# An FFT, mixing and feed-forward kernel: the first two chunks by halves of the features, eight weight blocks ahead, tables and third-stage inputs moved

## The chip, the cores and the metric

The kernel runs on one core of a Trainium2 chip. The metric is the device time of one launch in microseconds. PE is TensorE (PEld its weight loads), DVE is VectorE, ACT is ScalarE, POOL is GpSimd, SP is SyncE; SP, ACT and POOL each have a queue from which they issue DMAs in program order.

## The reference

```python
X = rfft(x, axis=1)                       # x: 8 batches, 3072 rows, 256 columns
Yr = Xr @ w_r - Xi @ w_i + b_r
Yi = Xr @ w_i + Xi @ w_r + b_i
Yr, Yi = soft_threshold(Yr, 0.01), soft_threshold(Yi, 0.01)
y = irfft(Yr + 1j * Yi, n=3072, axis=1)   # real, 8 x 3072 x 256
h = y.reshape(-1, 256) @ w_in             # 256 -> 2048
out = (h * tanh(softplus(h))) @ w_out     # 2048 -> 256
```

w_in and w_out arrive as float64.

## The kernel before

**Precision.** Each value of a product is split into a float32r part `hi` and a rest `lo`, and a product is three matmul passes (hi by hi, lo by hi, hi by lo). The split is one copy and one subtraction. float64 weights are read as raw words (`raw`) and turned into two such parts on DVE, in steps: the class `FromDouble` makes a block of 128 x 1024 values in nine DVE steps (lines 253 to 277), the last two of which run inside the next block's work. There are 16 blocks: eight of w_in (`w1(k, n)`, of features 512n to 512n+511) and eight of w_out (`w2(n)`, of feature blocks 2n and 2n+1).

**The transform, per batch.** Four stages pass through scratch memory in HBM:
- first stage, items a (7, two matmul steps each): tile `psa`, results `eva` stored;
- second stage, items b (12, `psb`, with a table `tt` from HBM) each followed by an item m (mixing by w_r and w_i, thresholds; two matmul steps, `psm` in batch 0, `psk` and `psp` later), results `y` stored;
- third stage, items c (13, `psc`), four input DMAs each;
- fourth stage, items f (12, `psf`, with a table `vt`), which give the feed-forward inputs `yh`, `yl` of one chunk for each pair of items.

`run_chain` is a generator that issues an item's `load`, table load `cload` and split `prep` some items ahead and gives back control after each matmul step; `cla` is how many items ahead the tables are. With `gap` set it also yields empty steps after a stage's loads and after its first preps.

**The feed-forward part.** 48 chunks (6 a batch) by 16 feature blocks make 768 steps t. `ffn1(t)` is six matmuls of 512 columns into `hp`, followed by Mish on ACT; `split_g` splits two steps' results into `gh` and `gl`; `ffn2(t - 4)` is eight matmuls into four accumulators `acc` of a chunk, which after 16 steps are added and stored. A chunk runs through all 16 feature blocks before the next one starts.

**The order.** It is written by hand, in program order per engine. Batch 0's transform runs first, with weight steps of DVE spread among its matmul steps (`PACE`, steps per matmul step by stage; `aux_steps` in `on_seg`, steps at a stage's start). Up to `N_EARLY` = 11 blocks, 97 steps, are made there, the rest at t 0 to 18. From t=0 on, each t also takes one step of `gen`, the next batch's transform up to its items f0 and f1, and of `extra`, a chain of one item f for the batch in hand, started at t%16 = 2 and 8. An empty step of `extra` leaves the t to `gen`; a matmul step does not. What is left of `gen` at a batch's last t is issued there in one go.

Before t=0 a job's weight load is issued on POOL from within an earlier job's steps, and its buffers go round among `raw`, `gl` and `ot` tiles. The loads of items c and f and of x are on SP; in batch 0 half of those of c are on POOL, and so is half of the stores of y.

Of the kernel before, what the change touches and what calls it, by code (L numbers as in the profile page):

```python
# [128 lines left out]
def fft_mix_ffn_kernel(ctx: ExitStack, tc: tile.TileContext, x, w_r, w_i, b_r, b_i, w_in, w_out,  # L129
# [147 lines left out]
            nc.vector.tensor_tensor(out=self.lo, in0=f32(self.high), in1=self.t, op=ALU.add)  # L277
            yield

    N_EARLY = 11  # L280

    def weight_jobs():
        def w1(k, n):
            sl = slice(n * 512, (n + 1) * 512)
            return (w_in.bitcast(I32)[k * 128:(k + 1) * 128, n * 1024:(n + 1) * 1024],
                    *(win[:, k, s, sl].rearrange("p (a c) -> p a c", a=2) for s in range(2)), False)

        def w2(n):
            return (w_out.bitcast(I32)[n * 256:(n + 1) * 256, :].rearrange("(k p) c -> p k c", p=128),
                    *(wout[:, 2 * n:2 * n + 2, s, :] for s in range(2)), True)  # L290

        order = [w1(0, 0), w1(1, 0), w1(0, 1), w1(1, 1), w2(0), w2(1), w1(0, 2), w1(1, 2), w2(2), w2(3),
                 w1(0, 3), w1(1, 3), w2(4), w2(5), w2(6), w2(7)]
        return [FromDouble(n, *a) for n, a in enumerate(order)]


# [399 lines left out]
    def run_chain(segs, ahead_n=3, ahead_a=2, cla=2, gap=0, hold=None, on_seg=None):  # L696


        for k, seg in enumerate(segs):
            while hold is not None and k == len(segs) - 1 and hold():  # L700
                yield None
            n = len(seg)
            at = [0, 0, 0]
            la, pla = (ahead_a, 1) if k == 0 and n == 7 else (ahead_n, 2)

            def ahead(i):
                for s, (d, f) in enumerate(((la, "load"), (cla, "cload"), (pla, "prep"))):
                    while at[s] < min(n, i + d):
                        getattr(seg[at[s]], f)()
                        at[s] += 1  # L710

            while at[1] < min(n, cla):
                seg[at[1]].cload()
                at[1] += 1
            while at[0] < min(n, la):
                seg[at[0]].load()
                at[0] += 1
            if on_seg is not None:
                on_seg(k)
            last = k == len(segs) - 1  # L720
            for _ in range(gap + (4 if k == 2 else 1 if last else 0) if gap else 0):
                yield None
            while at[2] < min(n, pla):
                seg[at[2]].prep()
                at[2] += 1
            for _ in range((2 if last or k == 1 else 1) if gap else 0):
                yield None
            for i in range(n):
                ahead(i + 1)
                for f in seg[i].mm:  # L730
                    tick()
                    f()
                    yield k
            tick()
# [2 lines left out]
    NCH = NB * 6  # L737
    s_t, g_t, acc = {}, {}, {}

    def ffn1(t):  # L740

        c, f = divmod(t, KFF)
        yh, yl = y_t[(c // 6, c % 6)]
        hp = ps_d.tile([128, 512], F32, tag="d", name="hp")
        n = 0
        for k in range(2):
            for s, m in ((0, yh), (0, yl), (1, yh)):
                nc.tensor.matmul(out=hp, lhsT=win[:, k, s, f * 128:(f + 1) * 128], rhs=m[:, k, :],  # L748
                                 start=n == 0, stop=n == 5)
                n += 1  # L750
        if t % 2 == 0:
            s_t[t // 2] = p_s.tile([128, 2, 512], F32, tag="s", name="s")
        nc.scalar.activation(out=s_t[t // 2][:, t % 2, :], in_=hp, func=ACTF.Mish)  # L753

    def split_g(q, early):
        s = s_t.pop(q)
        gh = p_g.tile([128, 2, 512], F32R, tag="gh", name="gh")
        gl = p_g.tile([128, 2, 512], F32R, tag="gl", name="gl", bufs=2)
        if early:
            nc.scalar.activation(out=gh, in_=s, func=ACTF.Copy)  # L760
        else:
            nc.vector.tensor_copy(out=gh, in_=s)  # L762
        nc.vector.tensor_tensor(out=gl, in0=s, in1=f32(gh), op=ALU.subtract)  # L763
        g_t[q] = (gh, gl)

    def ffn2(t):
        c, f = divmod(t, KFF)
        gh, gl = g_t[t // 2]
        if f == 0:
            acc[c] = [ps_o.tile([128, 2, 256], F32, tag="o", name=f"acc{k}") for k in range(4)]  # L770
        last = f == KFF - 1
        if last:
            ot = p_o.tile([128, 2, 2, 256], F32, tag="ot", name="ot")
        for k in range(4):
            b2, h = divmod(k, 2)
            p = acc[c][k]
            o = b2 * 256 + h * 128
            nc.tensor.matmul(out=p, lhsT=gh[:, t % 2, o:o + 128], rhs=wout[:, f], start=f == 0, stop=False)  # L778
            nc.tensor.matmul(out=p[:, 0], lhsT=gl[:, t % 2, o:o + 128], rhs=wout[:, f, 0], start=False, stop=last)  # L779
            if last:  # L780
                cor = p_w.tile([128, 256], F32, tag="cor", name="oc")
                nc.scalar.activation(out=cor, in_=p[:, 1], func=ACTF.Copy)  # L782
                nc.vector.tensor_tensor(out=ot[:, h, b2, :], in0=p[:, 0], in1=cor, op=ALU.add)  # L783
        if last:
            b, cc = divmod(c, 6)
            dst = out[b * SEQ:(b + 1) * SEQ].rearrange("(h a b2) c -> a h b2 c", h=2, b2=12)
            nc.sync.dma_start(out=dst[:, :, 2 * cc:2 * cc + 2, :].rearrange("a h b2 c -> a h (b2 c)"),
                              in_=ot.rearrange("p h b c -> p h (b c)"))
            acc.pop(c)
        if t % 2 == 1:  # L790
            g_t.pop(t // 2)


    with tc.manual_schedule():
# [22 lines left out]
        def aux_steps(m):  # L817
            for _ in range(m):
                if started[0] or n_aux[0] < 9 * N_EARLY - 2:
                    next(aux_gen, None)  # L820
                    n_aux[0] += 1

        def on_seg(k):
            if k == 1:
                top[0] = N_EARLY
                aux_load(4)
                setup_mix()
                aux_steps(6)
            elif k == 2:
                aux_steps(12)  # L830
            elif k == 3:
                aux_steps(10)

        PACE = (1.6, 0.9, 1.4, 2)
        first = chain(0)
        cnt = 0
        owed = 0.0
        for k in run_chain(first, ahead_n=6, ahead_a=3, cla=3, on_seg=on_seg):
            cnt += 1
            if cnt in (2, 6):  # L840
                aux_load(1 + (cnt > 2))
            if cnt == 8:
                load_mix()
                load_bias()
            if cnt == 11:
                for it in first[1][:3]:
                    it.cload()
            if cnt == 20:
                setup_u()
            if cnt == 57:  # L850
                for it in first[3]:
                    it.cload()
            if cnt > 4:
                owed += PACE[k]
            while owed >= 1:
                aux_steps(1)
                owed -= 1
# [9 lines left out]
        for t in range(NT + LAG):  # L867
            tt = t % NS
            b = t // NS
            if t == 0:  # L870
                aux_load(N_EARLY + 2)
            if t < 18:
                aux_steps(3)
            if t == 18:
                aux_steps(18)
                mix_gauss()
            if t < NT:
                if tt == 0:
                    gen = run_chain(chain(b + 1), gap=2, hold=lambda: hold[0]) if b + 1 < NB else None
                hold = [tt < 5 * KFF + 2]  # L880
                ffn1(t)
                c = tt // KFF
                if tt % KFF in (2, 8) and c < 5:
                    extra = run_chain([[item_f(b, 2 * c + 2 + (tt % KFF) // 8)]], gap=2)
            if t % 2 == 0 and t // 2 - 1 in s_t:
                split_g(t // 2 - 1, t < 18)
            did = None
            if extra is not None:
                did = next(extra, -1)
                if did == -1:  # L890
                    extra = did = None
            if did is None and gen is not None and t < NT:
                did = next(gen, -1)
                if did == -1:
                    gen = None
            if t < NT and tt == NS - 1 and gen is not None:
                hold = [False]
                for _ in gen:
                    pass
                gen = None  # L900
            if t >= LAG:
                ffn2(t - LAG)
# [26 lines left out]
```

## Time and profile before

| | |
|---|---|
| median of 3 runs | 2815.71 us (2812.26 to 2817.09) |
| profiled execution | 2812.9 us, span 2811.1 us |
| granted TensorE clock, mean | 0.987 |
| busy PE, DVE, ACT | 97%, 69%, 34% |
| first stage of batch 0 | 0 to 43 us |
| second | 43 to 106 us |
| third | 106 to 146 us |
| fourth | 146 to 158 us |
| first hp (t=0) | 158.19 us |

Stages are told apart by the lines of their instructions. A row of the timeline gives start and length in microseconds, engine, line, operation, tiles, and in brackets the idle time of that engine ahead of it and what ended it. PE's lengths overlap: the next matmul starts before the one before has ended. A row of the waits gives engine and tile, what was waited for, the sum in microseconds, the number of times and the longest.

### The profile page before, as it was taken

Reading aid. Unit: us, or ns where it says so; the run is one execution under the profiler, and the core shown is the slowest. Engines: PE = TensorE matmul, PEld = TensorE weight load, DVE = VectorE, ACT = ScalarE, POOL = GpSimd, SP = SyncE. Lnnn points to the kernel's source line nnn. Section 1 sums busy time; section 2 is a strip of 40 time slices with the busy share of each in tenths; the row PEclk is TensorE's granted clock in tenths of the full one; section 3 lists DMA queues with packets and bytes.
Section 4 is the critical chain, followed back from the end, with each engine's and each line's share of the span. In section 5 each row is a group of like instructions: output and inputs, shape, how many; then the busy total and the mean of one; then the engine's idle time right before and its main releaser. Section 6 shows DMA issues by size and latency. Waiting matters only on the chain.

```text
span 2811.1 us, 39281 instructions
## 1 busy us (share of the span) xinstructions
PE 2739.7 (97%) x14782; PEld 2333.5 (83%) x14782; DVE 1952.8 (69%) x3294; ACT 951.2 (34%) x1947; POOL 148.0 (5%) x274
## 2 busy tenths in 40 slices
PE   6779999999999999999999999999999999999999
PEld 5558888888888888888888888888888888888887
DVE  5788866778667776678766777567766778655553
ACT  4333333333333333333333333323333333333232
POOL 1400000000000000000000000000000000000000
PEclk9789999999999999999999999999999999999999
DMA  7643324333233323342233332433324333231000
GB/s 223 204 143 86 94 70 120 102 90 94 72 112 109 99 80 86 101 121 84 76 106 102 104 84 68 120 106 87 90 75 120 98 91 91 78 95 42 27 27 16
DMA packets 170388, 266.38 MB, mean 95 GB/s; under 512 B 22518, under 2 KB 67590, under 8 KB 170198
## 3 DMA queue, kind: packets, MB, share of 16 engines
q1 hardware_dynamic: 122806, 173.75, 20.6%
q0 software_dynamic: 33536, 64.95, 8.6%
q10 hardware_dynamic: 13856, 25.17, 3.1%
q8 instruction: 117, 1.92, 0.3%
q14 instruction: 73, 0.60, 0.1%
HBM read 163.10 MB, written 100.68 MB: 94 GB/s over the span
## 4 chain that ended last, share of the span: by engine, by line
PE 87%; DVE 5%; DMA 3%; SPq 2%; issue 1%; ACT 1%; POOL 0%; ACTq 0%; DVEq 0%; POOLq 0%
PE hp L748 35%; PE acc L778 23%; PE acc L779 12%; PE psp L518 4%; PE psa L345 2%; PE psc L626 2%; SPq L604 2%; PE psk L499 2%; PE psf L666 2%; PE psb L434 2%; DMA ld<-in_x_dram 1%; DMA ld<-s 1%; PE psf L667 1%; DVE lo L190 1%; PE psb L436 1%
## 5 line engine op out<-in xcount | busy, mean ns | idle before, releaser
L778 PE MATMUL acc<-wout,gh 128*128 128x512 f32 x3072 | 1115.7, 397 | 0.0
L748 PE MATMUL hp<-yh,win 128*128 128x512 f32 x3072 | 1082.1, 393 | 4.9 <-ACT yh L675 4.6
L753 ACT ACTIVATE s<-hp 128x512 f32<-128x512 f32 x768 | 458.5, 597 | 1368.7 <-PE hp L748 1283.3
L779 PE MATMUL acc<-wout,gl 128*128 128x256 f32 x3072 | 859.2, 280 | 0.0
L748 PEld LDWEIGHTS hp<-yh,win 128*128 128x128 f32 x3072 | 578.6, 188 | 137.4 <-ACT yh L675 4.8
L778 PEld LDWEIGHTS acc<-wout,gh 128*128 128x128 f32 x3072 | 576.6, 188 | 123.4 <-issue 6.0
L748 PE MATMUL hp<-yl,win 128*128 128x512 f32 x1536 | 604.1, 393 | 0.0
L779 PEld LDWEIGHTS acc<-wout,gl 128*128 128x128 f32 x3072 | 577.5, 188 | 16.3
L763 DVE TENSOR_TENSOR gl<-s,gh 128x1024 fp32r<-128x1024 f32 x384 | 470.5, 1225 | 65.3 <-PE acc L779 26.1
L762 DVE CAST gh<-s 128x1024 fp32r<-128x1024 f32 x376 | 258.7, 688 | 207.1 <-ACT s L753 207.1
L748 PEld LDWEIGHTS hp<-yl,win 128*128 128x128 f32 x1536 | 289.2, 188 | 35.0 <-DVE yl L676 0.4
L190 DVE TENSOR_TENSOR lo<-ld,hi 120x512 fp32r<-120x512 f32 (+3 forms) x390 | 269.7, 692 | 31.8 <-ACT hi L189 16.3
L187 DVE CAST hi<-ld 120x512 fp32r<-120x512 f32 (+2 forms) x367 | 154.7, 422 | 56.5 <-DMA ld<-s 55.5
L670 DVE TENSOR_TENSOR eo<-psf,cor 128x256 f32<-128x256 f32 x192 | 76.9, 422 | 117.5 <-ACT cor L669 116.8
L783 DVE TENSOR_TENSOR ot<-acc,oc 128x256 f32<-128x256 f32 x192 | 72.8, 420 | 98.2 <-ACT oc L782 98.2
L650 POOL DMA_DIRECT2D vt<-in_c_v_dram x96 | 52.5, 547 | 1609.4 <-PE psf L667 1261.1
L518 PE MATMUL psp<-wmix,xh 128*128 128x256 f32 x672 | 133.2, 281 | 0.0
L676 DVE TENSOR_TENSOR yl<-yt,yh 128x512 fp32r<-128x512 f32 x96 | 66.5, 693 | 67.1 <-ACT yh L675 67.1
L518 PEld LDWEIGHTS psp<-wmix,xh 128*128 128x128 f32 x672 | 109.1, 188 | 3.6
L675 ACT ACTIVATE yh<-yt 128x512 fp32r<-128x512 f32 x96 | 60.7, 632 | 145.4 <-DVE yt L673 145.4
L626 PE MATMUL psc<-hi,uu 120*120 120x512 f32 (+1 forms) x224 | 89.0, 412 | 17.2 <-ACT hi L189 14.8
L666 PE MATMUL psf<-vt,hi 128*128 128x256 f32 x384 | 95.4, 325 | 7.5 <-ACT hi L189 7.5
(114 smaller groups left out, 2630.5 us busy)
## 6 DMA issues: line engine op xcount, KB each, us to landing
ld<-s SPq DMA_DIRECT2D x185, 256.0 KB
tt<-in_c_t_dram POOLq DMA_DIRECT2D x104, 256.0 KB, 3.2
vt<-in_c_v_dram POOLq DMA_DIRECT2D x96, 256.0 KB, 3.0
out_dram<-ot SPq DMA_DIRECT2D x48, 512.0 KB
ld<-in_x_dram SPq DMA_DIRECT2D x90, 240.0 KB
s<-ev ACTq DMA_DIRECT2D x89, 240.0 KB
s<-y SPq DMA_DIRECT2D x330, 64.0 KB
ld<-s SPq DMA_DIRECT2D x350, 60.0 KB
```

Source lines behind the costliest of these rows:

```text
L187: nc.vector.tensor_copy(out=hi, in_=src)
L190: nc.vector.tensor_tensor(out=lo, in0=src, in1=f32(hi), op=ALU.subtract)
L518: nc.tensor.matmul(out=it.ps[:, ri * 256:(ri + 1) * 256], lhsT=m[:, c, 130 - ri * 128:258 - ri * 128], rhs=wmix[:, c, s, 2 * ri, :], start ...
L626: nc.tensor.matmul(out=ps[:K, sl], lhsT=uu[:K, var, s, :K], rhs=m[:K, sl], start=n == 0, stop=n == 2)
L666: nc.tensor.matmul(out=ps[:, p], lhsT=it.hi[:, q:q + 128], rhs=it.v[:, p], start=True, stop=False)
L670: nc.vector.tensor_tensor(out=eo[:, c], in0=ps[:, :, 0], in1=cor, op=ALU.add)
L748: nc.tensor.matmul(out=hp, lhsT=win[:, k, s, f * 128:(f + 1) * 128], rhs=m[:, k, :], start=n == 0, stop=n == 5)
L753: nc.scalar.activation(out=s_t[t // 2][:, t % 2, :], in_=hp, func=ACTF.Mish)
L762: nc.vector.tensor_copy(out=gh, in_=s)
L763: nc.vector.tensor_tensor(out=gl, in0=s, in1=f32(gh), op=ALU.subtract)
L778: nc.tensor.matmul(out=p, lhsT=gh[:, t % 2, o:o + 128], rhs=wout[:, f], start=f == 0, stop=False)
L779: nc.tensor.matmul(out=p[:, 0], lhsT=gl[:, t % 2, o:o + 128], rhs=wout[:, f, 0], start=False, stop=last)
```

## The change

- The first two chunks (t 0 to 31) take turns: features 0 to 7 of chunk 0, 0 to 7 of chunk 1, 8 to 15 of chunk 0, 8 to 15 of chunk 1. Both use a two-accumulator form of `ffn2`, with 12 matmuls of 256 columns and no addition at the end.
- Eight weight blocks (70 steps) are made ahead of t=0, in an order that holds all of features 0 to 7. The other 76 steps stand at t 0 to 25.
- In batch 0's transform tables are loaded five items ahead, not three.
- Items f2 and f3 of batch 0 form one chain at t=0, f4 and f5 one at t=24. Batch 1's chain starts at t=18 and takes one more step at every fifth t behind 26. The Gauss weights of later batches (`mix_gauss`) are made at t=30, not 18.
- In `run_chain` the third stage has two empty steps after its first preps, not one. The same line gives a chain of one single stage (the items f of `extra`) one empty step after its prep, not two.

```diff
-    N_EARLY = 11
+    N_EARLY = 8
-        order = [w1(0, 0), w1(1, 0), w1(0, 1), w1(1, 1), w2(0), w2(1), w1(0, 2), w1(1, 2), w2(2), w2(3),
-                 w1(0, 3), w1(1, 3), w2(4), w2(5), w2(6), w2(7)]
+        order = [w1(0, 0), w1(1, 0), w1(0, 1), w1(1, 1), w2(0), w2(1), w2(2), w2(3),
+                 w1(0, 2), w1(1, 2), w2(4), w1(0, 3), w1(1, 3), w2(5), w2(6), w2(7)]
...
-            for _ in range((2 if last or k == 1 else 1) if gap else 0):
+            for _ in range((2 if k else 1) if gap else 0):
                 yield None
...
+    def place(t):
+        if t < 2 * KFF:
+            q, r = divmod(t, KFF // 2)
+            return q % 2, q // 2 * (KFF // 2) + r
+        return divmod(t, KFF)
...
+    def ffn2_two(t, c, f, gh, gl, last):
+        if f == 0:
+            acc[c] = [ps_o.tile([128, 2, 256], F32, tag="o", name=f"acc{k}") for k in range(2)]
+        ot = p_o.tile([128, 2, 2, 256], F32, tag="ot", name="ot") if last else None
+        for b2 in range(2):
+            for h in range(2):
+                o = b2 * 256 + h * 128
+                p = acc[c][b2][:, h, :]
+                for n, (m, s) in enumerate(((gh, 0), (gh, 1), (gl, 0))):
+                    nc.tensor.matmul(out=p, lhsT=m[:, t % 2, o:o + 128], rhs=wout[:, f, s, :],
+                                     start=f == 0 and h == 0 and n == 0, stop=last and h == 1 and n == 2)
+            if last:
+                nc.scalar.activation(out=ot[:, :, b2, :], in_=acc[c][b2], func=ACTF.Copy)
+        return ot
...
-                aux_steps(6)
+                aux_steps(8)
             elif k == 2:
                 aux_steps(12)
             elif k == 3:
-                aux_steps(10)
-        PACE = (1.6, 0.9, 1.4, 2)
+                aux_steps(9)
+        PACE = (1.6, 0.45, 0.7, 2)
-        for k in run_chain(first, ahead_n=6, ahead_a=3, cla=3, on_seg=on_seg):
+        for k in run_chain(first, ahead_n=6, ahead_a=3, cla=5, on_seg=on_seg):
...
-                for it in first[1][:3]:
+                for it in first[1][:5]:
                     it.cload()
...
-            if t < 18:
-                aux_steps(3)
-            if t == 18:
-                aux_steps(18)
+            if t < 26:
+                aux_steps(2 if t < 8 else 4 if t < 16 else 3)
+            if t == 30:
                 mix_gauss()
             if t < NT:
-                if tt == 0:
+                if tt == (0 if b else 18):
                     gen = run_chain(chain(b + 1), gap=2, hold=lambda: hold[0]) if b + 1 < NB else None
...
-                if tt % KFF in (2, 8) and c < 5:
+                if t in (0, 24):
+                    extra = run_chain([[item_f(0, 2 + t // 12), item_f(0, 3 + t // 12)]], gap=2)
+                elif t >= 2 * KFF and tt % KFF in (2, 8) and c < 5:
                     extra = run_chain([[item_f(b, 2 * c + 2 + (tt % KFF) // 8)]], gap=2)
             if t % 2 == 0 and t // 2 - 1 in s_t:
-                split_g(t // 2 - 1, t < 18)
+                split_g(t // 2 - 1, t < 26)
+            if b == 0 and gen is not None and t % 5 == 4 and t > 26:
+                next(gen, None)
```

On POOL, in batch 0's second stage (numbers tell tiles apart; `tt` are tables, the first one here is block 2's; `s3<-y` are stores, `raw` is a weight load), before:

```order
L400 DMA tt_453<-in_c_t_dram 128x512
L400 DMA tt_517<-in_c_t_dram 128x512
L205 DMA uu_103<-in_c_u_dram 120x720
L564 DMA s3_164<-y_534 32x512 x2
L400 DMA tt_568<-in_c_t_dram 128x512
L564 DMA s3_164<-y_584 32x512 x2
L245 DMA raw_594<-in_moe_w_in_dram 128x1024
L400 DMA tt_619<-in_c_t_dram 128x512
```

and after:

```order
L400 DMA tt_408<-in_c_t_dram 128x512
L400 DMA tt_456<-in_c_t_dram 128x512
L400 DMA tt_519<-in_c_t_dram 128x512
L205 DMA uu_103<-in_c_u_dram 120x720
L564 DMA s3_164<-y_535 32x512 x2
L400 DMA tt_568<-in_c_t_dram 128x512
L564 DMA s3_164<-y_584 32x512 x2
```

Block 5's table (tt_619 before, tt_568 after) now stands behind one pair of stores instead of two and behind no weight load. In the third stage two `raw` stood between the loads of c on POOL before; after, one stands ahead of them all and two behind the stage's `vt`.

On PE, at item f10 in a later batch (`psf` is its product; `gh_7503` before and `gh_7607` after are the halves of the same two steps t), before:

```order
L778 MATMUL acc3_7510<-wout_110,gh_7503 128x512
L779 MATMUL acc3_7510<-wout_110,gl_7504 128x256
L748 MATMUL hp_7560<-yh_7021,win_109 128x512
L748 MATMUL hp_7560<-yl_7022,win_109 128x512
L748 MATMUL hp_7560<-yh_7021,win_109 128x512 x2
L748 MATMUL hp_7560<-yl_7022,win_109 128x512
L748 MATMUL hp_7560<-yh_7021,win_109 128x512
L666 MATMUL psf_7571<-vt_7452,hi_7527 128x256
L667 MATMUL psf_7571<-vt_7452,lo_7528 128x128
```

and after:

```order
L755 MATMUL hp_7643<-yl_7089,win_109 128x512
L755 MATMUL hp_7643<-yh_7088,win_109 128x512
L666 MATMUL psf_7659<-vt_7556,hi_7631 128x256
L667 MATMUL psf_7659<-vt_7556,lo_7632 128x128
L666 MATMUL psf_7659<-vt_7556,hi_7631 128x256
L667 MATMUL psf_7659<-vt_7556,lo_7632 128x128
L666 MATMUL psf_7667<-vt_7556,hi_7631 128x256
L667 MATMUL psf_7667<-vt_7556,lo_7632 128x128
L666 MATMUL psf_7667<-vt_7556,hi_7631 128x256
L667 MATMUL psf_7667<-vt_7556,lo_7632 128x128
L797 MATMUL acc0_7611<-wout_110,gh_7607 128x512
```

psf stood behind the acc group that reads these halves first and behind one more hp; now it stands ahead of both, one t earlier. Its load's place on SP, behind the first three c items' loads, is the same.

On PE, at the end of batch 0 (from the end of item f1's psf of batch 1 to the next hp), before:

```order
L667 MATMUL psf_4804<-vt_4646,lo_4715 128x128
L778 MATMUL acc0_4573<-wout_110,gh_4706 128x512
L779 MATMUL acc0_4573<-wout_110,gl_4707 128x256
L778 MATMUL acc1_4574<-wout_110,gh_4706 128x512
L779 MATMUL acc1_4574<-wout_110,gl_4707 128x256
L778 MATMUL acc2_4575<-wout_110,gh_4706 128x512
L779 MATMUL acc2_4575<-wout_110,gl_4707 128x256
L778 MATMUL acc3_4576<-wout_110,gh_4706 128x512
L779 MATMUL acc3_4576<-wout_110,gl_4707 128x256
L748 MATMUL hp_4825<-yh_4078,win_109 128x512
```

and after:

```order
L667 MATMUL psf_4945<-vt_4824,lo_4893 128x128
L797 MATMUL acc0_4599<-wout_110,gh_4847 128x512
L798 MATMUL acc0_4599<-wout_110,gl_4848 128x256
L797 MATMUL acc1_4600<-wout_110,gh_4847 128x512
L798 MATMUL acc1_4600<-wout_110,gl_4848 128x256
L797 MATMUL acc2_4601<-wout_110,gh_4847 128x512
L798 MATMUL acc2_4601<-wout_110,gl_4848 128x256
L797 MATMUL acc3_4602<-wout_110,gh_4847 128x512
L798 MATMUL acc3_4602<-wout_110,gl_4848 128x256
L755 MATMUL hp_4966<-yh_4912,win_109 128x512
```

Before, that hp still reads the old chunk (yh_4078), and the new one follows two t later; after, it reads yh_4912, which f0 and f1 write, and both their psf stand right ahead of this acc group.

More of the change, by code (lines that the diff above doesn't have):

```diff
@@ L738, in fft_mix_ffn_kernel @@
     s_t, g_t, acc = {}, {}, {}
+    def place(t):
[3 more added lines that the diff above has]
+        return divmod(t, KFF)
     def ffn1(t):
-        c, f = divmod(t, KFF)
+        c, f = place(t)
         yh, yl = y_t[(c // 6, c % 6)]
@@ L764, in split_g, with ffn2_four @@
         g_t[q] = (gh, gl)
-    def ffn2(t):
-        c, f = divmod(t, KFF)
-        gh, gl = g_t[t // 2]
+    def ffn2_two(t, c, f, gh, gl, last):
[12 more added lines that the diff above has]
+        return ot
+    def ffn2_four(t, c, f, gh, gl, last):
         if f == 0:
             acc[c] = [ps_o.tile([128, 2, 256], F32, tag="o", name=f"acc{k}") for k in range(4)]
-        last = f == KFF - 1
-        if last:
-            ot = p_o.tile([128, 2, 2, 256], F32, tag="ot", name="ot")
+        ot = p_o.tile([128, 2, 2, 256], F32, tag="ot", name="ot") if last else None
         for k in range(4):
@@ L783, in ffn2 @@
                 nc.vector.tensor_tensor(out=ot[:, h, b2, :], in0=p[:, 0], in1=cor, op=ALU.add)
+        return ot
+    def ffn2(t):
+        c, f = place(t)
+        gh, gl = g_t[t // 2]
+        last = f == KFF - 1
+        ot = (ffn2_two if c < 2 else ffn2_four)(t, c, f, gh, gl, last)
         if last:
```

## The prediction

> **What bounds the kernel now.** I read the page first, then busy time by stage, then the waits of PE in each stage, and last the timeline where a wait stood. The page and the busy time by stretch (its columns: length, then busy time and number for PE, PEld, DVE, ACT and POOL, granted clock, DMA share, GB/s):
>
> ```profile
> PE 2739.7 (97%) x14782; PEld 2333.5 (83%) x14782; DVE 1952.8 (69%) x3294; ACT 951.2 (34%) x1947; POOL 148.0 (5%) x274
> 106.00:146.00 40.00, 22.40 (x42) 9.95 (x42) 27.07 (x51) 17.02 (x30) 19.66 (x35) 0.54 0.73 216
> 158.20:240.00 81.80, 70.90 (x323) 55.19 (x324) 72.66 (x127) 32.20 (x55) 5.47 (x9) 0.96 0.41 114
> 240.00:340.00 100.00, 100.00 (x595) 88.56 (x594) 79.02 (x143) 36.24 (x83) 7.05 (x13) 1.00 0.33 95
> ```
>
> From 240 us on PE is never out of work: it is the bound, and its work is hardly changed. So the change can win only what PE loses before 240 us and in the few waits behind it, and it loses whatever new wait it puts into a stretch that is dense now. I go through the places in order of time; "lost" means the delay of PE's next start. Each idle time that the profile shows understates it by about 0.25 us, because a matmul's modelled end lies 0.16 us behind the next possible start and the matmul after a wait runs about 0.1 us longer.
>
> **Tables five items ahead.** In the second stage PE's work of a block follows without a gap, but for the tables:
>
> ```profile
> PE psb L422 <- DMA tt<-in_c_t_dram: 2.2, 2, 1.5
> 68.50 0.56 POOL L245 DMA_DIRECT2D raw<-in_moe_w_in_dram  x1
> 69.06 0.56 POOL L400 DMA_DIRECT2D tt<-in_c_t_dram  x1
> 76.00:78.00 2.00, 2.00 (x6) 0.50 0.58 152
> ```
>
> Block 5's table is issued at 69.06, behind a weight load and behind a store that waits for DVE. After the change it stands one store earlier on POOL, some 5 us, and that weight load is gone from there. Both waits (2.2, lost 2.5) should go. After the first PE ran at half clock around 77 us, for about 3.4 us: 1.7 more. Taken: -4.0; bounds 0 and -4.2. The fourth table loaded at the very start takes 256 KB of busy DMA there and gives it back at 38 us: 0.
>
> **Weights, third stage.** DVE loses 27 of 97 steps before the feed-forward part, but in the second stage PE was the one that had no gaps, so DVE's relief is worth nothing there. In the third stage the inputs' arrival decides. Two weight loads of 512 KB leave the POOL queue between the inputs; one moves to the front of the stage, and the first two of the feed-forward part can start towards its end:
>
> ```profile
> 114.23 0.82 POOL L245 DMA_DIRECT2D raw<-in_moe_w_out_dram  x1
> 116.08 0.65 POOL L245 DMA_DIRECT2D raw<-in_moe_w_in_dram  x1
> 108.00:110.00 2.00, 0.00 (x0) 0.50 0.37 93
> 120.00:122.00 2.00, 1.48 (x3) 0.50 0.95 346
> 112.86 0.63 ACT L189 ACTIVATE hi<-ld 120x512 fp32r<-120x512 f32 x1 [2.97 <-DMA ld<-s]
> 136.11 0.63 ACT L189 ACTIVATE hi<-ld 120x512 fp32r<-120x512 f32 x1 [0.48 <-DVE lo L190]
> 137.70 0.63 ACT L189 ACTIVATE hi<-lds 120x512 fp32r<-120x512 f32 x1 [0.47 <-DVE lo L190]
> 139.75 0.61 ACT L189 ACTIVATE hi<-ld 120x512 fp32r<-120x512 f32 x1
> ```
>
> Thirteen inputs take 26.9 us from 112.86 to 139.75, 2.24 each; late in the stage, where they lie ready, it is 1.6 (136.11 to 137.70). At 1.6 all twelve steps take 19.2, so at most 7.7 us can be won; if the bytes only move, nothing. The load at the front falls where DMA is 0.37 busy, the two late ones meet the last inputs and all late stores. I take half: -4 (bounds 0 and -7.7). The Trainium skill (DMA: Bandwidth & Descriptors, Issuing engines are not separate DMA queues) says that DMAs of all issuers interleave on the same 16 engines. By that a moved weight load saves nothing where the stage's bytes stay the same, and the sum would be 4 us higher; the trace has both full and half idle stretches in this stage.
>
> In the fourth stage two weight steps run on DVE between the two items:
>
> ```profile
> 154.87 0.69 DVE L264 SCALAR_TENSOR_TENSOR dt<-raw,dt 128x512 int32<-128x512 int32 x1
> 155.59 0.43 DVE L267 TENSOR_SCALAR raw<-dt 128x512 int32<-128x512 int32 x1
> 155.93 0.75 DVE L670 TENSOR_TENSOR eo<-psf,cor 128x256 f32<-128x256 f32 x2
> ```
>
> They are gone there, as all 70 early steps are used up: 155.93 - 154.87 = -1.0, on the path to the first hp.
>
> **The first 30 steps of the feed-forward part.** Before, DVE is nearly full (72.66 of 81.8) with weight steps and the next batch's first stage at once, and PE waits. The larger waits, and the first gl of DVE:
>
> ```profile
> PE psa L345 <- DVE raw L269: 3.2, 1, 3.2
> PE psa L345 <- DVE hi L187: 2.9, 2, 1.9
> PE psa L345 <- DVE eo L670: 2.6, 1, 2.6
> PE psa L345 <- DVE eva L354: 1.0, 1, 1.0
> 167.08 1.23 DVE L763 TENSOR_TENSOR gl<-s,gh 128x1024 fp32r<-128x1024 f32 x1 [2.78 <-ACT gh L760]
> ```
>
> With three small ones of 1.2 the waits make 10.9 in nine pieces, so about 12.9 us lost. After: t 0 to 19 carry no first stage, and DVE needs at most four steps (2.2 us by starts such as 154.87 to 155.59) and half a gl (0.6) a t, beside 2.8 of PE. Three waits remain. At t=4 psf stands behind gl, two steps and a split on DVE: gl starts 8.9 us after the first hp as now, so psf comes 11.8 after it where PE is ready at 9.9; with its lo 2.4 lost. At t=21 the first psa waits for a split queued behind a gl: 1.1. At t=32 psa waits behind the Gauss weights and a gl: 1.5. Together 5.0, so -7.9 (bounds -10 and -3). Weight halves are ready 4 us or more ahead of use. One matmul group of the two-accumulator form is 12 of 256 columns, like psp; the four-accumulator form lasts from 757.36 to 758.75:
>
> ```profile
> 261.72 1.43 PE psp L518 x12
> 757.36 0.40 PE L778 MATMUL acc<-wout,gh 128*128 128x512 f32 x1
> 758.75 0.39 PE L748 MATMUL hp<-yh,win 128*128 128x512 f32 x1
> ```
>
> 1.43 against 1.39, 32 times: +1. The DVE adds that the last one saves are off the path: 0.
>
> **The later batch.** Batch 1's stages start at t=18, not 0, and get an extra step every fifth t. They catch up only in the last t: f0 and f1 both stand at t=95, right ahead of the hp that reads them. One such chain in the dense part:
>
> ```profile
> 583.16 0.29 PE L666 MATMUL psf<-vt,hi 128*128 128x256 f32 x1
> 584.26 0.81 DVE L670 TENSOR_TENSOR eo<-psf,cor 128x256 f32<-128x256 f32 x2 [2.40 <-ACT cor L669]
> 586.57 0.69 DVE L676 TENSOR_TENSOR yl<-yt,yh 128x512 fp32r<-128x512 f32 x1 [0.70 <-ACT yh L675]
> ```
>
> yh is done where yl starts, 3.4 us after psf; the second item's eo starts behind the first yl (4.0) and its yh is done 2.3 later, at 6.3; PE has 1.9 of psf and 1.4 of acc to do. 3.0 lost on yh, 0.5 on yl: +3.5, once. At the other six boundaries f1 moves one t later; its psf then starts 5.2 us ahead of that hp, whose yh needs 3.4: 0. The doubled steps bring DVE to about 84% in batch 0: +0.5 (0 to 3).
>
> **The item f with one empty t less.** Items f outside the chain now run one t (hp and acc, 760.13 - 757.36 = 2.77 us) sooner after their split. In the dense part their halves are ready more than one t ahead, but for one kind. That is item 10 of each batch, whose load sits on SP behind twelve issues of the third stage (SP, DVE, PE):
>
> ```profile
> 745.44 9.67 SPq L604 DMA_DIRECT2D ld<-s  x12
> 755.16 0.56 SPq L644 DMA_DIRECT2D ld<-s  x1
> 758.76 0.43 DVE L187 CAST hi<-ld 128x512 fp32r<-128x512 f32 x1 [5.04 <-DMA ld<-s]
> 759.22 0.69 DVE L190 TENSOR_TENSOR lo<-ld,hi 128x512 fp32r<-128x512 f32 x1
> 760.13 0.29 PE L666 MATMUL psf<-vt,hi 128*128 128x256 f32 x1
> 760.26 0.22 PE L667 MATMUL psf<-vt,lo 128*128 128x128 f32 x1
> 2442.61 0.69 DVE L190 TENSOR_TENSOR lo<-ld,hi 128x512 fp32r<-128x512 f32 x1
> 2443.54 0.29 PE L666 MATMUL psf<-vt,hi 128*128 128x256 f32 x1
> ```
>
> lo ends at 759.91 and its matmul would want to start at 760.26 - 2.77 = 757.49: lost 759.91 + 0.15 - 757.49 = 2.6 us. Nothing ahead of the load moves in batches 1 to 6, so the data are no earlier. The last of the six (2442.61, 2443.54) gives the same 2.6; over the six, whose spare time varies by 0.9, it is 15.4. In batch 0 the load now comes ahead of the third stage: 0. Bounds 12 and 17, or 0 if the load is earlier. On DVE gl and eo stand behind that split, and acc needs that gl only two t later.
>
> **Third stage, later batches.** The one more empty t takes away these waits:
>
> ```profile
> PE psc L626 <- DVE hi L187: 2.3, 6, 0.5
> PE psc L626 <- DVE lo L190: 1.2, 7, 0.2
> ```
>
> 3.5 in 13 pieces, lost 6.9, and 0.3 at one psf: -7.2.
>
> **Sum.** -4.0 - 4 - 1.0 - 7.9 + 1 + 3.5 + 0.5 + 15.4 - 7.2 = -3.7 us. The profiled execution took 2812.9, so it would be 2809.2; the runs' median, 2815.71, lies 2.8 above that execution, so 2812.0 for the median. What this kernel's measurement can tell from no change is about 0.2%, 5.6 us: 2810.1 to 2821.3 is the same.
>
> **Rivals.** (B) Item 10's load arrives in time, or PE comes later there: then -3.7 - 15.4 = -19.1, 2796.6. For it: six of its spare times depend on one queue; against: DVE idles 5 us for that load in each batch. (C) The front wins half: third stage 0 as the bytes stay, and the feed-forward start keeps 9 of 12.9: -3.7 + 4 + 4 = +4.3, 2820.0. For it: DVE there is filled again with steps and gl. (D) Slower: each new wait of about 2.5 us ends in a window of half clock, as the wait of 1.5 us at 73.91 did: 1.7 us each at seven places, +11.9, so +8.2, 2823.9. It decides if six or more of the seven do so. Against: the waits of 3.2 and 2.6 us in the feed-forward start left the clock full. The Trainium skill (TensorE: Matmul & The Clock Gate, What's actually happening) gives about one idle window of 3.4 us as what drops the clock; by that D is out and the sum stays, but the row at 76 us shows a drop after less.
>
> **Numbers.** As summed 0.55, B 0.15, C 0.20, D 0.10. As summed reaches from 2802 to 2821 (unknown third stage and feed-forward start, each 3 to 4 us), a third of it below 2810.1: 0.18. Faster 0.18 + 0.15 = 0.33; slower D and a little of C, 0.11; same 0.56. The range 2797 to 2822 leaves out half of B, most of D and the end of C.
>
> **What would show it.** In the changed trace: no tt wait of psb and no half clock in the second stage; first hp at 149 (152 if C); under 6 us lost between it and t=34; one hp waiting 3 us for yh near 500 us; psf waiting 2 us for hi and 0.5 for lo six times, once a batch; no psc wait. I am wrong at the largest term if psf shows no wait in the third stage.

## The result and the profile after

The changed kernel took 2830.82 us (median of 6 runs, 2826.27 to 2836.77) against 2815.82 of the kernel before: ratio 1.0054, interval 1.0043 to 1.0064, so 15 us slower. Forecast were 2812.0, with 2822 as the upper end. The profiled execution took 2834.8 us, 4 above its median, and that of before 2812.9, 3 below its median; the two traces so differ by 21.9 us, 7 more than the medians.

The page of the changed kernel:

```profile
PE 2753.8 (97%) x14910; PEld 2349.2 (83%) x14910; DVE 1940.2 (68%) x3282; ACT 957.1 (34%) x1947; POOL 146.2 (5%) x274
```

Its busy time by stretch, in the columns and the stretches that were shown of before:

```profile
106.00:146.00 40.00, 21.44 (x42) 9.93 (x42) 22.66 (x40) 16.77 (x30) 18.63 (x34) 0.54 0.77 237
158.20:240.00 81.80, 79.20 (x485) 69.90 (x484) 67.76 (x116) 35.77 (x57) 5.76 (x10) 1.00 0.31 94
240.00:340.00 100.00, 96.87 (x570) 84.41 (x568) 81.91 (x147) 36.71 (x81) 5.82 (x11) 0.98 0.37 106
```

The start of the feed-forward part looks as it was meant to: PE is busy 79.2 of 81.8 us, not 70.9. But from 240 us on, where PE had no gap, it now has them, and the clock is no longer 1.00 throughout. PE's busy time rose by 14.1 us. That is hardly the 128 matmuls more of the two-accumulator form: run 11 below, with the same matmuls, has 2739.4, as before had. For the most part it is matmuls at half clock: seven windows of half clock begin behind the first hp, of about 1.6 us more each, where the kernel before has none. The waits of PE from the first hp on (in the second row, 3.5 is the wait of the first hp itself):

```profile
PE psf L666 <- DVE hi L187: 10.3, 6, 2.0
PE hp L755 <- ACT yh L675: 6.4, 2, 3.5
PE psf L667 <- DVE lo L190: 2.7, 8, 0.3
PE psc L626 <- DVE hi L187: 2.1, 2, 1.6
PE psa L345 <- DVE eva L354: 1.8, 2, 1.2
```

The first row is item f10, once in each of batches 1 to 6, as forecast. The first of the six, on SP, DVE and PE:

```profile
747.71 9.68 SPq L604 DMA_DIRECT2D ld<-s  x12
757.42 0.56 SPq L644 DMA_DIRECT2D ld<-s  x1
760.73 0.43 DVE L187 CAST hi<-ld 128x512 fp32r<-128x512 f32 x1 [4.76 <-DMA ld<-s]
759.38 0.39 PE L755 MATMUL hp<-yh,win 128*128 128x512 f32 x1
761.21 0.39 PE L666 MATMUL psf<-vt,hi 128*128 128x256 f32 x1 [1.44 <-DVE hi L187]
761.94 0.33 PE L667 MATMUL psf<-vt,lo 128*128 128x128 f32 x1 [0.34 <-DVE lo L190]
763.56 0.63 PE L797 MATMUL acc<-wout,gh 128*128 128x512 f32 x1
```

The load stands behind twelve issues on SP as before, and psf waits for hi and lo. The last row was not forecast as the likeliest: an acc matmul of 0.63, where 0.40 is usual, so half clock behind the wait. The wait of hp at t=96, with its acc behind it, is the same picture:

```profile
505.45 0.50 PE L755 MATMUL hp<-yh,win 128*128 128x512 f32 x1 [2.88 <-ACT yh L675]
506.17 0.50 PE L755 MATMUL hp<-yl,win 128*128 128x512 f32 x1 [0.22 <-DVE yl L676]
508.00 0.63 PE L797 MATMUL acc<-wout,gh 128*128 128x512 f32 x1
```

**Where the 21.9 us of the traces lie.** The hp rows of the timeline, six matmuls a t, divide a trace into three parts: first hp (t=0), from there to t=100, from t=100 to t=767.

| kernel | first hp | to t=100 | to t=767 |
|---|---|---|---|
| before | 158.19 | 359.03 | 2280.33 |
| changed | 154.24 | 365.17 | 2300.07 |
| forecast difference | -9.0 | -3.9 | +9.2 |
| measured difference | -3.95 | +6.14 | +19.74 |

(The forecast's -7.2 for the third stage is split here into 1.0 for the one of batch 0's feed-forward part and 6.2 for the six later ones.) All three parts are worse than forecast.

### The profile page after: what moved, and what is told of

It is laid out like the page before. It is cut to its first block, busy times and chain, and to the rows that moved or that the text cites. A ratio compares the mean times of both kernels' runs of the same rounds, so it can differ in the third digit from the quotient of the medians.

```text
span 2833.0 us, 39500 instructions
## 1 busy us (share of the span) xinstructions
PE 2753.8 (97%) x14910; PEld 2349.2 (83%) x14910; DVE 1940.2 (68%) x3282; ACT 957.1 (34%) x1947; POOL 146.2 (5%) x274
## 3 DMA queue, kind: packets, MB, share of 16 engines
q8 instruction: 118, 1.93, 0.3%
## 4 chain that ended last, share of the span: by engine, by line
PE 88%; DMA 4%; DVE 3%; SPq 3%; ACT 1%; issue 1%; POOL 0%; ACTq 0%; DVEq 0%; POOLq 0%
PE hp L755 34%; PE acc L797 23%; PE acc L798 11%; PE psp L518 4%; SPq L604 2%; PE psa L345 2%; PE psc L626 2%; PE psk L499 2%; PE psf L666 2%; PE psb L434 2%; PE psm L535 1%; PE acc L783 1%; DMA ld<-s 1%; PE psf L667 1%; DMA ld<-in_x_dram 1%; DMA s<-eva 1%
## 5 line engine op out<-in xcount | busy, mean ns | idle before, releaser
L797 PE MATMUL acc<-wout,gh 128*128 128x512 f32 x2944 | 1074.3, 398 | 0.0
L798 PE MATMUL acc<-wout,gl 128*128 128x256 f32 x2944 | 826.2, 281 | 0.0
L797 PEld LDWEIGHTS acc<-wout,gh 128*128 128x128 f32 x2944 | 555.2, 189 | 118.1 <-issue 5.2
L798 PEld LDWEIGHTS acc<-wout,gl 128*128 128x128 f32 x2944 | 556.1, 189 | 15.8
L666 PE MATMUL psf<-vt,hi 128*128 128x256 f32 x384 | 98.1, 329 | 23.4 <-DVE hi L187 10.3
L473 DVE TENSOR_TENSOR y<-psp,y 128x512 f32<-128x512 f32 x84 | 58.0, 691 | 73.9 <-PE psp L518 72.4
L354 DVE TENSOR_TENSOR eva<-psa,s2nd 120x512 f32<-120x512 f32 (+1 forms) x98 | 64.1, 685 | 62.4 <-DMA s<-eva 41.6
```

Source lines behind the costliest of these rows:

```text
L666: nc.tensor.matmul(out=ps[:, p], lhsT=it.hi[:, q:q + 128], rhs=it.v[:, p], start=True, stop=False)
```

## Experiments

The times are medians; each ratio is against runs of the kernel before on the same chip. "Lost at f10" means the time from hp of a batch's 64th t to that of its 86th, less the same stretch of the first run below, which has no wait there.

**1. The second empty t given back to the extra items.**

```diff
-            for _ in range((2 if k else 1) if gap else 0):
+            for _ in range((2 if last or k else 1) if gap else 0):
```

> The changed kernel with the second empty t given back to the chains of one segment (the extra items f); the third stage keeps its second empty t. If the waits of item f10 and the half-clock windows behind them are the loss (in the changed kernel's trace 6 waits of psf that delay PE 2.5 us each, four of them followed by a window of half clock of 1.6 us: 15.1 + 6.4 = 21.5), the six psf waits are gone and the time falls by 15 to 22 us, to about 2810 to 2816; the wait of hp at t=96 stays. If f10 has little to do with it and the loss stands in the start of the feed-forward part and at the first batch boundary, the time falls by less than 5 us, to 2826 or more.

2813.89 us, ratio 0.9995 (0.9986 to 1.0004): 16.9 us below the changed kernel, inside the 15 to 22. From 520 us on PE waits for nothing that the profile shows; the part of the trace that this covers, t=100 to 767, takes 2274.83, 25.2 less than in the changed kernel: 21.7 at f10, and 2.8 in psa waits for `eva` at the starts of later batches, which I had not priced and which also need the missing empty t. But two waits came up near t=30 to 32:

```profile
PE hp L755 <- DVE eva L354: 3.8, 1, 3.8
PE hp L755 <- ACT s L760: 3.3, 1, 3.3
```

The second pair of extras of batch 0 (t=24) is now one t later, and hp of t=32 reads what it makes.

**2. The same line alone, in the kernel before.**

```diff
-            for _ in range((2 if last or k == 1 else 1) if gap else 0):
+            for _ in range((2 if k else 1) if gap else 0):
```

> The kernel before with that one line of the change alone. My prediction's terms: +15.4 for f10 and -7.2 for the third stage, +8.2 us. With a window of half clock behind each f10 wait that falls into one window (two thirds of six, 1.6 each) +14 to +18. If the waits come only with the rest of the change: -7.

2838.7 us, ratio 1.0082 (1.0068 to 1.0096), +23 and above all I expected. From t=100 on its trace is 17.3 us longer than that of before, as the theory with half clock has it (+14 to +18). The rest stands ahead of t=100: an extra item of batch 0, whose psf starts 0.1 us after its hi is ready and where the profile names ACT's s2nd as what came last (second row), and in the second stage, whose code this kernel shares with the one before, more was lost than there (third row; 2.2 before):

```profile
PE psf L666 <- DVE hi L187: 12.4, 7, 2.4
PE psf L666 <- ACT s2nd L350: 5.4, 1, 5.4
PE psb L422 <- DMA tt<-in_c_t_dram: 3.7, 2, 1.9
```

**3. Another rule for the doubled steps.** On top of run 1:

```diff
-            if b == 0 and gen is not None and t % 5 == 4 and t > 26:
+            if b == 0 and gen is not None and t % 3 == 2 and 26 < t < 72:
```

> The first of these runs and also another rule for batch 1's doubled steps: every third t from 29 to 71 instead of every fifth from 29 on, so that none falls into its third stage and f0 and f1 stand at t=92 to 94 instead of both at 95. If the wait of hp at t=96 (3.0 + 0.5 us and a window of half clock, 5.3 in all) and the psc waits near 476 us (4.7 with their window) come from that rule, this one is 8 to 10 us faster than the first run and has neither; if the doubled steps cost elsewhere what they save there (DVE nearly full near t=30 to 70), the two are within 3 us.

2808.71 us, ratio 0.9975 (0.9966 to 0.9984): 5.2 below run 1, where 8 to 10 were expected. The psc waits of batch 1's third stage are gone; the hp wait at t=96 shrank from 2.9 to 1.0 and has no half clock behind it, but is not gone.

**4. The waits filled with matmuls of no use.** In the changed kernel, nine ahead of f10's psf and twelve ahead of hp at t=96. The condition `if b` also holds in batch 7, beyond the six batches of the expectation; there no later batch's loads stand ahead of f10's, and psf has no wait:

```diff
+                if b and nb == 10 and c == 0:
+                    for _ in range(9):
+                        nc.tensor.matmul(out=ps, lhsT=wout[:, 0, 0, :128], rhs=wout[:, 0], start=True, stop=True)
...
+        if t == 6 * KFF:
+            for _ in range(12):
+                nc.tensor.matmul(out=hp, lhsT=wout[:, 0, 0, :128], rhs=wout[:, 0], start=True, stop=True)
```

> The changed kernel with matmuls of no use put where PE waits: nine of 512 columns ahead of item f10's psf in batches 1 to 6 (1.9 us of a wait of 2.2) and twelve ahead of the first hp of t=96 (2.6 us of 3.0). The waits themselves last as long; only PE is busy in them. If windows of half clock behind these waits cost what the trace shows (five windows of 1.6 us), the time falls by 6 to 8 us and the trace has none there; if the half-clock windows are no part of the loss, the time stays within 2 us of the changed kernel's or rises.

2829.99 us, ratio 1.0055 (1.0042 to 1.0068): 0.8 below the changed kernel, so by the medians the expectation of 6 to 8 failed. The trace shows full clock at all seven places; at the first:

```profile
758.00:766.00 8.00, 6.69 (x37) 5.34 (x36) 6.06 (x11) 1.89 (x4) 0.53 (x1) 1.00 0.43 134
```

PE there, with the nine of the filling and the wait that is left:

```profile
756.28 2.21 PE L666 MATMUL psf<-wout 128*128 128x512 f32 x9
759.45 0.38 PE L670 MATMUL psf<-vt,hi 128*128 128x256 f32 x1 [0.96 <-DVE hi L187]
```

Lost at f10 were 3.9, 2.5, 2.3, 3.6, 2.6, 2.5 (17.4), against 21.7 in the changed kernel. In the first and the fourth batch hi came 1.6 and 0.6 us later than in the changed kernel's trace, which gave back what the clock saved. And in batch 7 the filling fills no wait, but adds 2.1 us (the nine, and psf right behind them):

```profile
2742.57 2.21 PE L666 MATMUL psf<-wout 128*128 128x512 f32 x9
2744.62 0.28 PE L670 MATMUL psf<-vt,hi 128*128 128x256 f32 x1
```

So some 3 us were won at the filled places by the medians, 0.8 and these 2.1, which is still not 6 to 8. Whether the filling causes the later hi, and what half clock costs in a median run, stays open; the traces say 4.3 and (against that of run 5) 5.6 us at f10.

**5. The changed kernel once more, for a second trace.**

> The changed kernel once more, unedited, for a second trace. If a wait brings a window of half clock only where most of it falls into one window of the clock's own 3.41 us, and these windows stand at another phase in each execution, the six waits of psf are the same 2.5 us each but the windows of half clock follow others of them than before (2, 3, 4 and 5 of the six there had none for the second and the sixth), and the time changes by 1.5 us for each. If a property of the place decides, the same four have them.

2831.75 us, with the same sums of psf waits, 10.3 in six pieces for hi. Lost at f10 by batch, with the windows of half clock behind:

| batch | 1 | 2 | 3 | 4 | 5 | 6 |
|---|---|---|---|---|---|---|
| first trace | 3.9, one | 2.7, none | 4.1, one | 4.5, one | 4.1, one | 2.5, none |
| second trace | 2.6, none | 2.4, none | 4.2, one | 4.0, one | 4.2, one | 5.5, two |

So the place alone doesn't decide: batches 1 and 6 differ between the traces. Without half clock a wait costs 2.55 (mean of four), with one window 4.15 (seven): 1.6 more. The windows of half clock start at multiples of 3.413 us from each other (506.75 and 762.75 in the first trace: 75 of them). Cut along this grid, the first two batches of the first trace read (length, PE busy, ..., third from the end the clock):

```profile
759.34:762.75 3.41, 1.64 (x10) 1.01 (x10) 1.88 (x4) 0.82 (x2) 0.00 (x0) 1.00 0.57 210
762.75:766.16 3.41, 3.41 (x12) 2.93 (x12) 2.68 (x6) 1.18 (x3) 0.53 (x1) 0.50 0.61 154
1097.26:1100.67 3.41, 2.48 (x13) 1.75 (x11) 0.00 (x0) 0.94 (x2) 0.00 (x0) 1.00 0.66 181
1100.67:1104.08 3.41, 2.23 (x14) 1.91 (x15) 2.91 (x5) 0.77 (x2) 0.53 (x1) 1.00 0.37 109
1104.08:1107.50 3.42, 3.42 (x19) 2.94 (x18) 2.69 (x7) 1.12 (x2) 0.00 (x0) 1.00 0.52 135
```

In batch 1 the whole wait lies in one window, PE is idle for 1.77 of it, and the next window has half clock. In batch 2 the same wait lies across a border, 0.93 and 1.18, and the clock stays. The second trace, batches 1 and 6:

```profile
753.83:757.25 3.42, 1.69 (x9) 1.10 (x7) 0.53 (x2) 0.60 (x1) 0.00 (x0) 1.00 0.81 241
757.25:760.66 3.41, 3.07 (x18) 2.62 (x19) 3.27 (x6) 0.77 (x2) 0.53 (x1) 1.00 0.34 88
2453.67:2457.09 3.42, 1.49 (x7) 0.90 (x6) 0.59 (x2) 0.60 (x1) 0.00 (x0) 1.00 0.76 245
2457.09:2460.50 3.41, 3.16 (x12) 2.67 (x13) 3.27 (x6) 0.77 (x2) 0.53 (x1) 0.50 0.29 81
```

1.73 idle kept the clock, 1.93 did not.

**6. The empty t kept at the start.** Run 3, but the two chains of two items (t=0, t=24) have one empty t as in the changed kernel:

```diff
-            for _ in range((2 if last or k else 1) if gap else 0):
+            for _ in range((2 if k else empty if last else 1) if gap else 0):
```

> The run with the other catch-up rule once more, but the two chains of two items that start at t=0 and t=24 keep their one empty t as in the changed kernel; the single extra items from t=32 on have two. In the runs with two everywhere PE lost 8 us between t=28 and t=34, where the fifth item f of batch 0 is computed too late for the hp of t=32 that reads it. If that is what the second empty t costs there, this kernel is 5 to 6 us faster than the run with the catch-up rule (2808.7): 2802 to 2804. If those waits are DVE's fill and only change their name, it is within 2 us of it.

2803.71 us, ratio 0.9960 (0.9947 to 0.9973): 5.0 below run 3, and the hp waits near t=30 are gone.

**7. The second pair of extras at t=20.** Run 3, with `if t in (0, 20)`.

> The run with the catch-up rule (two empty t everywhere), the second pair of items f started at t=20 instead of 24. If only the order matters, the hp of t=32 has its input four t earlier and PE waits neither there nor for psf near 250 us: 2800 to 2802, 1 to 3 us below the run that keeps the changed kernel's start. If DVE, which has three weight steps a t up to t=25, is the limit, the waits move ahead to t=23 to 28 and the time is 2804 to 2808.

2802.90 us, ratio 0.9952 (0.9938 to 0.9966). Not to be told from run 6: hp's wait at t=32 shrank to 0.4, but hp waits at t=8, as in run 3, for the first pair, which has two empty t there.

**8. Tables alone**, in the kernel before:

```diff
-        for k in run_chain(first, ahead_n=6, ahead_a=3, cla=3, on_seg=on_seg):
+        for k in run_chain(first, ahead_n=6, ahead_a=3, cla=5, on_seg=on_seg):
...
-                for it in first[1][:3]:
+                for it in first[1][:5]:
```

> The kernel before with only the tables five items ahead (and five at the start). My term was -4.0 of 2815.5, so 2811.5. The kernel before lost 4.3 us in the second stage in its profiled execution (two waits and one window of half clock) and about 10 in another execution of the same code, which had two such windows: by that the mean gain is 4 to 7 us. If the tables only wait elsewhere, within 1 us of no change.

2809.71 us, ratio 0.9980 (0.9971 to 0.9989): -5.8. No wait for tt is left. The second stage, first psb to last psm, took 53.35 us, against 56.76 in the trace of before and 62.43 in that of run 2.

**9. Two parts alone: tables and the third stage's empty t**, in the kernel before. Run 8 and

```diff
-            for _ in range((2 if last or k == 1 else 1) if gap else 0):
+            for _ in range((2 if last or k else 1) if gap else 0):
```

> The kernel before with two of the parts alone: tables five items ahead, and a second empty t for the third stage (the extra items keep theirs). If these two are all that the change can win, the parts add up: the tables alone gave 2809.7, the third stage's psc waits are 0.9 us a batch over six batches, 5.5: 2804.2, within 2 us of the two versions that also take the first two chunks in turns, spread the weights otherwise and start batch 1 later (2802.9 and 2803.7). If the start by turns is worth the 6 to 7 us of my prediction, this kernel stays at 2808 or above.

2803.97 us, ratio 0.9958 (0.9945 to 0.9970), 0.2 from the sum. So the rest of the change (turns of the first chunks, fewer weight blocks ahead, the later batch 1), even where its own stalls are taken away as in runs 6, 7 and 10, is worth 0.3 to 1.5 us by the medians of runs 6, 7 and 10, which can't be told from nothing. The start of the feed-forward part in this kernel:

```profile
158.20:240.00 81.80, 72.52 (x333) 57.14 (x332) 71.65 (x125) 31.15 (x54) 5.48 (x9) 0.96 0.42 120
240.00:340.00 100.00, 100.00 (x598) 88.70 (x597) 79.69 (x144) 36.92 (x85) 7.28 (x13) 1.00 0.33 90
```

And in run 6:

```profile
158.20:240.00 81.80, 79.20 (x487) 70.00 (x486) 68.18 (x117) 36.44 (x58) 5.43 (x9) 1.00 0.32 95
240.00:340.00 100.00, 96.33 (x572) 83.65 (x572) 82.73 (x148) 35.66 (x79) 6.37 (x12) 0.98 0.38 108
```

Run 6 gains 6.7 us of busy PE up to 240 us, loses 3.7 in the next stretch, and has the work of batch 1 that it put off still ahead of it. It reaches t=100 in 359.09 us from its first hp, and the kernel with two parts in 357.64.

**10. One empty t for the first pair, the second pair at t=20.** Runs 6 and 7 together.

> The best version so far (catch-up rule, second pair of items f at t=20) with one empty t instead of two for the first pair alone, at t=0. In its trace hp waited 2.5 us at t=8 for that pair, with a window of half clock of 1.5 behind it; the version with one empty t there lost about 1.1 at that place. If nothing else moves: 2802.9 - 3 = 2799 to 2801. If the clock's phase in the run decides more than that, it is not to be told from 2802.9.

2802.43 us, ratio 0.9951 (0.9938 to 0.9965): the lowest median, but not to be told from run 7. Hp's wait at t=8 is gone, but psf waits at t=4 in its place (1.5 for hi and 0.3 for lo), as in run 6.

**11. Item f10's load ahead of the third stage's on SP.** The changed kernel with

```diff
-                elif t >= 2 * KFF and tt % KFF in (2, 8) and c < 5:
+                elif t >= 2 * KFF and tt % KFF in ((0, 8) if c == 4 else (2, 8)) and c < 5:
```

> The changed kernel with item f10 started two t earlier in each batch (at the 64th t instead of the 66th), so that its load stands on SP ahead of the twelve loads of the third stage; it keeps its one empty t. If its place on that queue is what makes it late (twelve issues of 0.8 us each, 9.7 us, stand ahead of it in the trace), the six waits of psf and the windows of half clock behind them are gone as with the second empty t given back: 2809 to 2812, 19 to 22 us below the changed kernel. If the missing empty t is the cause and not the queue, the halves are as late as before relative to psf: the six waits stay, 2829 or more.

2810.35 us, ratio 0.9986 (0.9977 to 0.9995): 20.5 below the changed kernel. With one empty t, but ahead of the twelve issues, no psf wait is left from t=100 on. The stretch around the first f10 here:

```profile
756.00:768.00 12.00, 12.00 (x62) 10.14 (x61) 6.98 (x11) 3.22 (x6) 0.00 (x0) 1.00 0.12 35
```

And in the changed kernel:

```profile
756.00:768.00 12.00, 10.22 (x46) 8.31 (x45) 5.07 (x9) 3.19 (x6) 0.53 (x1) 0.86 0.44 128
```

## Why the prediction was wrong, step by step

The measured median lies 18.8 us above the forecast. Three steps of the sum failed: half clock behind the new waits stood in it at nothing, with rival D at 0.10; the gain of the third and fourth stage was counted without the wait between them; and that of the first 30 steps without the stretches that receive the work put off.

- **Item f10, +15.4: the wait right, its cost too small.** The waits are where and as long as forecast (2.55 each without half clock, so 15.3). The step that failed is the one that set rival D at 0.10: that waits of 3.2 and 2.6 us in the start had left the clock full. Cut along the grid, the longer of these (203.21 to 206.38) lies across a border of it, and so does the other (1.44 and 1.13 to each side of 215.27):

```profile
201.62:205.03 3.41, 1.59 (x8) 0.98 (x6) 3.34 (x6) 0.00 (x0) 0.00 (x0) 1.00 0.00 0
205.03:208.45 3.42, 2.07 (x10) 1.77 (x11) 2.87 (x6) 3.04 (x5) 0.00 (x0) 1.00 0.75 222
```

  That the clock stayed full there was luck of the phase, and proved nothing for the new waits. D was priced at seven windows of 1.7; the trace has seven windows behind the first hp, of 1.6 each, four of them behind f10, the others near 250, 479 and 507 us. That the number is the same is chance: those near 250 and 479 stand at waits that D didn't count. Run 11, which takes f10's waits and the half clock behind them away and leaves the rest, is 20.5 us faster by the medians: that is what f10 cost, not 15.4. The Trainium skill (TensorE: Matmul & The Clock Gate, What's actually happening) says that the window of some 3.4 us runs free and doesn't start with the kernel. The traces agree: the grid's first border stands 1.58 us behind the first instruction in the first trace of the changed kernel and 2.90 in the second. I had used only its "idle window" and had ruled D out by it, where 1.9 us of idle time in one window are enough.
- **The missing empty t costs more than f10:** 2.8 us of psa waits for `eva` at the starts of later batches, which are there in the changed kernel (both traces) and in run 11 (2.9), and not in run 1. I had looked only at the halves that extra items split, not at the batch that begins beside them.
- **Third stage, later batches, -7.2: right.** Run 9 against run 8, with that edit alone, is -5.7 by medians and -6.0 in the traces from t=100 on, where 6.2 was the forecast's part.
- **Tables, -4.0: right in kind, perhaps too small.** -5.8 by medians. The trace of before held two waits and one window of half clock; another execution of the same stage (run 2) held two windows and lost 5.7 more. The bound "0 to -4.2" took one execution for all.
- **Third and fourth stage, -5.0: wrong in sum.** From the last psm to the first hp the four traces with the old weight order take 53.2 to 54.9 us (mean 54.0), the nine with the changed one 52.6 to 54.0 (mean 53.1): -1.0. In the means, psc itself, first to last, is 3.1 us shorter (28.2 to 25.1), near the 4 taken, and the fourth stage, from its first psf to hp, 1.1 shorter, as forecast. But between them psf starts 2.8 us later behind the last psc (7.2 to 10.0; in the two main traces 7.54 and 9.99), and that step stood in the sum at nothing. The stage's last store on ACT and the first load of an item f on SP, before (two rows) and after (two rows):

```profile
142.99 0.32 ACTq L629 DMA_DIRECT2D s<-ev  x1
145.56 0.56 SPq L644 DMA_DIRECT2D lds<-s  x1
137.64 0.32 ACTq L629 DMA_DIRECT2D s<-ev  x1
142.78 0.56 SPq L644 DMA_DIRECT2D lds<-s  x1
```

  The load comes 5.1 us after that store now, not 2.6. Two weight loads and two more tables are now issued just ahead of the stage's last stores, where before it was one weight load; that they hold the stores up fits, but no run shows it alone. The Trainium skill (DMA: Bandwidth & Descriptors, Issuing engines are not separate DMA queues) says that DMAs of all issuers interleave on the same 16 engines. What the prediction drew from that, that a moved load saves nothing, came out for the two stages together: only the fourth stage's own -1.1 is left.
- **The start of the feed-forward part, -7.9 + 1: wrong as a sum.** PE's delays between the first hp and t=34 fell from 13.2 to 7.7, so 5.5 of 7.9 came. The waits at t=4 and t=21 are as forecast (2.4 and 1.2 lost), but the third was mis-sized: the second pair of extras and the psa beside it lose 4.1 at t=28 and 29, where 1.5 stood for one psa. The two-accumulator form is 0.06 us a t slower, 1.9 in all. And what was put off came back. The doubled steps fall into batch 1's third stage, which runs beside batch 0's feed-forward part; there psc waits with half clock behind them cost 4.7 (forecast: a gain of 1.0), and the hp wait at t=96 was 3.5 as forecast, with 1.7 of half clock on top. Run 9, which has the old start, is as fast as the versions with the new one: the forecast counted the waits of one stretch and not the work that came back in the next.

As a whole: of the miss of 25.6 us between the traces' difference and the forecast of -3.7, about 11 are half clock in seven windows, 4 the third and fourth stage, 3 the psa waits, and the rest the start and the tables: up to the last psm the changed trace is 2.4 shorter, not 4.0 (in run 5's trace of the same kernel 4.7).

By the medians f10 is the smaller part of the miss. Run 11 without f10's loss is 5.2 us below the kernel before, where the forecast without its +15.4 has 19.1 (rival B's 2796.6). So of the 18.8 us between the measured median and the forecast, 5 stand at f10 and nearly 14 are gains that did not come. In run 11's trace 2.4 of them lie ahead of the first hp, 7.4 from there to t=100, with two windows of half clock among them, and 4.3 behind, most of that the psa waits.

## What to carry to other kernels

A wait of PE of 2 to 3 us in a dense part costs its length, and by chance another 1.6 us for the clock: count both, and never take one execution as evidence that the clock holds. An item whose load is issued behind another stage's loads has that queue's length (here twelve issues, 9.7 us) as part of its lead; before an empty step is taken away, look for the one item whose lead is shorter than the others', or move its load ahead of the queue. And work that is put off out of a crowded stretch is only won if the stretch that receives it has room: two small parts alone were as fast as every version of the whole change that was run.

## What the runs showed of the hardware

In the twelve traces of the changed kernel and its variants and that of before, the stretch from 165 us on was cut along the clock's grid of 3.413 us. Of windows at full clock with 1.9 us or more in which the profile shows PE idle, 22 of 22 were followed by half clock; of those with 1.35 to 1.9, 11 of 25; of those with 0.6 to 1.35, 1 of 64. So the idle time of one window counts, and not the length of the wait alone or its place in the program: the wait of 3.2 us above, split 1.82 and 1.34, did nothing, and the f10 wait of batch 3 in the first trace, 1.63 for hi and 0.34 for lo in one window, did. Between 1.35 and 1.9 us it doesn't settle the outcome: windows with 1.38 were followed by half clock, one with 1.85 was not. What else counts there stays open.
